# Window attention, block pipeline: the q and k matmuls of the convolution slots uncut

## The chip, the cores and the metric

The kernel runs on one core of a Trainium2 chip. A core has TensorE (PE, with its weight loads shown as PEld), VectorE (DVE), ScalarE (ACT), GpSimd (POOL) and SyncE (SP, which here only issues DMAs). The metric is the device time of one execution in microseconds.

## The reference

The input is an image of 511 x 511 tokens with 192 channels in bf16. A depthwise 3x3 convolution of it is added to it, the result is normalised over the channels, and windows of 7 x 7 tokens go through attention with 4 heads of 48 channels; the projected output is added to the image after the convolution.

```python
    for i in range(kk):
        for j in range(kk):
            pe = pe + xp[:, i:i + H, j:j + W, :] * dw_pe[i, j][None, None, None, :]
    x0 = x + pe
    h = _layernorm(x0, axis=-1)
    ...
    qkv = (hw @ w_qkv).reshape(-1, ws * ws, 3, nh, dh)
    ...
    attn = jnp.einsum('wnhd,wmhd->whnm', q, k) * scale
    attn = _softmax(attn, axis=-1)
    out = jnp.einsum('whnm,wmhd->wnhd', attn, v)
    out = out.reshape(-1, ws * ws, C) @ w_o
    ...
    return x0 + out
```

There are 73 x 73 windows.

## The kernel before

**Blocks and slots.** The windows are cut into 42 blocks of up to 128. A block is worked in slots of 8 windows (`CH = 8`, 49 tokens each, `TOK = 392`), 16 slots for a full block, 667 in all. While the slots of block b run their attention, the same slots also convolve block b+1, normalise and transpose it, and project block b-1 out. The order of all this is written out by hand in the loop at lines 561 to 665 of `fast`; no scheduler changes it, and each engine runs its instructions in that order, waiting on semaphores.

**One slot** has these stages on PE, in this order:

- A, q (line 378, `stage_A`): the transposed tokens `HO` of 8 windows are multiplied by the two halves of the head-padded `Wqk`, with 96 + 96 channels accumulated in two matmuls (`kt`). ACT copies the result to `q` (386).
- E (461, `stage_E`): the attention output of two slots earlier is transposed back; DVE copies it to `HO` (462).
- A, k: as for q, with ACT's copy to `k`.
- V (394, `stage_V`): eight matmuls of 192 columns, ACT copies to `v` (402).
- projections (473, `proj`) of block b-1, two or three in each of slots 2 to 6: eight matmuls of 192 columns each, a copy on ACT to `pO` (484), an addition to `X` on POOL (488).
- D (437, `stage_D`): attention weights times v of the previous slot; DVE normalises (446, 447).
- B (416, `stage_B`): the logits; ACT takes the exponential into `pt` (424).
- in later slots, transposes of the normalised rows of block b+1 (354), copied to `HO` by DVE or ACT (364).

All of A, E, V, D, B and the projections take their PSUM tile in turn from one rotation of three (`PS`), so a stage can start only when the copy out of the tile three uses back is done.

**The convolution** (`conv_mm`, 314 to 324) is one matmul per channel: the 81 values of a window's padded 9 x 9 patch for 128 windows are the stationary operand (`XP`, one channel out of 192, so its elements lie 192 apart), and 49 columns of a filter matrix `T` stream through. Every ten channels DVE adds the PSUM tile (one of two, `psc`) to `X` (324). These matmuls are not a stage of their own. They are placed between the matmuls of A and V by `fill(weight)` (597): each call adds a share of the slot's quota and issues as many convolution matmuls as the quota allows. A whole slot has weight 24: 8 for q, 8 for k, 8 for v. The quota of a block's 192 channels is spread over its first seven slots, 27 or 28 channels in each of the first six and 7 in the seventh. When the next block's convolution is finished and its loads are issued, the last slot convolves 20 channels of the block after that "ahead" (`ahead`, 590), placed by `fill` in the k and v stages.

**The cut.** In a slot with convolution left to do, and not in an "ahead" slot, `stage_A` issues each of its four products as two matmuls of 196 columns (`cuts = 2`, line 594), with `fill(1)` after each. In all others it issues one of 392 columns with `fill(2)` after it. The weights of a product are loaded again for the second half, since the two accumulation steps (`kt`) alternate.

**Loads and stores.** SP issues the patches `XP` of block b+2 once the convolution of block b+1 is done (there is one `XP`), then the tokens `X` of block b+2 (255) into the tile that block b-1 has left, and the stores of block b-1 (303) between them.

Of the kernel before, what the change touches and what calls it, by code (L numbers as in the profile page):

```python
# [32 lines left out]
WS, NH, C, DH, S = 7, 4, 192, 48, 49  # L33
BLK, CH, KP, KT = 128, 8, 81, 96
TOK = CH * S
# [27 lines left out]
class _Kernel:  # L63
# [194 lines left out]
    def fast(self, ctx):  # L258
# [4 lines left out]
        HO = [pool.tile([128, 2, BLK, 64], BF, name=f"HO{i}") for i in range(2)]  # L263
# [26 lines left out]
        mm = nc.tensor.matmul  # L290

        def two_bank(ps, ncol):
            return ps[:].rearrange("p (b n) -> p b n", b=2)[:, :, 0:ncol]
# [20 lines left out]
        def conv_mm(cv):  # L314
            c = cv.c
            if c % 10 == 0:
                cv.ps = PCB.next()
            mm(cv.ps[:, (c % 10) * S : (c % 10 + 1) * S], lhsT=XP[0:KP, :, c], rhs=T[0:KP, c, :], start=True, stop=True)  # L318
            cv.c += 1
            if cv.c % 10 == 0 or cv.c == C:  # L320
                c0 = c - c % 10
                n = cv.c - c0
                xv = self.X[cv.b % 3][:, :, c0 : c0 + n]
                nc.vector.tensor_tensor(out=xv, in0=cv.ps[:, 0 : n * S].rearrange("p (c s) -> p s c", s=S), in1=xv, op=ALU.add)  # L324
# [43 lines left out]

        def stage_A(b, ck, which, fill, cuts=1):
            dst = (q_, k_)[which]
            ps = PS.next()
            m = CH // cuts
            for ab in range(2):
                for i in range(cuts):
                    for kt in range(2):
                        mm(  # L378
                            ps[:, ab * 512 + i * m * S : ab * 512 + (i + 1) * m * S],
                            lhsT=self.Wqk[kt][0:KT, which * 2 + ab, :],  # L380
                            rhs=HO[b % 2][0:KT, kt, ck * CH + i * m : ck * CH + (i + 1) * m, 0:S],
                            start=(kt == 0),
                            stop=(kt == 1),
                        )
                        fill(2 / cuts)
            nc.scalar.copy(out=dst[:, :, 0:TOK], in_=two_bank(ps, TOK))  # L386

        def stage_V(b, ck, fill, eng, v_):
            ps = PS.next()
            for pi in range(4):  # L390
                w = ck * CH + 2 * pi
                col = (pi // 2) * 512 + (pi % 2) * C
                for kt in range(2):
                    mm(  # L394
                        ps[:, col : col + C],
                        lhsT=HO[b % 2][0:KT, kt, w : w + 2, :].rearrange("p w s -> p (w s)"),
                        rhs=self.Wv[kt][0:KT, :],
                        start=(kt == 0),
                        stop=(kt == 1),
                    )  # L400
                    fill(1)
            eng(  # L402
                out=v_[:].rearrange("p (b j) h e -> p b (j h) e", b=2)[:, :, :, 0:DH],
                in_=two_bank(ps, 2 * C).rearrange("p b (g d) -> p b g d", d=DH),
            )
# [142 lines left out]
        n = Next(0)  # L548
# [12 lines left out]
        for g in range(NG + LE + 1):  # L561
            b, ck = groups[g] if g < NG else (NB, g - NG)
# [5 lines left out]
            if ck == 0:  # L568
                n = nn if nn else Next(b + 1) if b + 1 < NB else None
# [9 lines left out]
            def part(lo, hi, total, at=None):  # L579
                return min(total, max(0, int(((f if at is None else at) - lo) / (hi - lo) * total + 0.5)))  # L580
# [7 lines left out]
            conv = n.conv if n else None  # L588
            conv_goal = base + part(0.0, 0.39 + d, C - base)
            ahead = n and conv.c == C and n.tr == WS and early and xpn == len(xp) and xln == len(xl)  # L590
            if ahead:
                conv, conv_goal = nn.conv, 10 * part(0.875, 1.0, 2)
            conv_start = conv.c if n else 0
            cuts = 2 if n and conv.c < conv_goal and not ahead else 1
            quota = [0.0]

            def fill(weight):
                quota[0] += (conv_goal - conv_start) * weight / (16 if ahead else 24)
                while n and quota[0] >= 0.999 and conv.c < conv_goal:
                    quota[0] -= 1.0  # L600
                    conv_mm(conv)
# [4 lines left out]
            def hook(share):  # L606

                nonlocal xpn, xln
                at = f0 + (f - f0) * share
                if n and n.conv.c == C:  # L610
                    n.stats(int(s_start + (s_goal - s_start) * share))
                while sq and sq[0][0] <= g + share:
                    _, bb, k = sq.pop(0)
                    store(bb, k)
                    stored[bb] = k + 1
                if n is None or n.conv.c == C:
                    goal = part(0.38 + d, 0.96 if many else 0.66 + 0.5 * d, len(xp), at)
                    while xpn < goal:
                        xp[xpn]()
                        xpn += 1  # L620
                    if b < 1 or stored.get(b - 1, 0) == len(CHUNKS):
                        goal = part(0.62 - 0.5 * d, 0.82, len(xl), at)
                        while xln < goal:
                            xl[xln]()
                            xln += 1

            if g < NG:
                stage_A(b, ck, 0, fill if not ahead else lambda w: None, cuts)
            if 0 <= g - LE < NG:
                stage_E(*groups[g - LE], nc.vector.tensor_copy)  # L630
            if g < NG:
                hook(0.3)
                stage_A(b, ck, 1, fill, cuts)
                hook(0.5)
                stage_V(b, ck, fill, nc.scalar.copy, vv[g % 2])
                while n and conv.c < conv_goal:
                    conv_mm(conv)
                hook(0.7)
# [275 lines left out]
```

## Time and profile before

| | |
|---|---|
| median of three runs | 3874.21 us (3873.48 to 3881.06) |
| the profiled execution | 3874.21 us, span 3872.5 us |
| mean granted TensorE clock | 0.938 |
| matmuls of 196 columns in A (line 378) | 4688 |
| matmuls of 392 columns in A (line 378) | 2992 |
| convolution matmuls (line 318) | 8064 |

One execution is profiled. Each instruction is shown with its engine, its line, and its tiles as written<-read. A matmul's length is modelled and includes its way through the array, so matmuls overlap in the listing; the distance between the starts of two tells how long the first one held the engine. A weight load may run beside the matmul before it. "Granted clock" is the share of TensorE's full speed that it was given. A wait is put down to the instruction that ended last before it. In an answer by intervals each line has the interval and its length, then busy time and number of instructions of PE, PEld, DVE, ACT and POOL, the granted clock, the busy share of the DMA engines and GB/s.

### The profile page before, as it was taken

To read this page: it belongs to the slowest core of one execution; us is meant where nothing else is said; L and a number is where in the kernel's file an instruction comes from. 1 tells how busy PE (TensorE), PEld (TensorE's weight loads), DVE (VectorE), ACT (ScalarE), POOL (GpSimd) and SP (SyncE) were. 2 spreads that over 40 slices of the span, in tenths; PEclk is the share of its full clock that TensorE was granted. 3 is DMA by queue.
4 is the path that set the end of the run, shared out by engine and by line. 5 is a ranking of instruction groups with operands and counts; after the bars stand their busy time and mean duration, and the time that the engine had idled before them with its cause. 6 is when DMAs were issued, how large, how long until landed. Compare 5 with 4: busy or idle time off the path is not lost.

```text
span 3872.5 us, 170289 instructions
## 1 busy us (share of the span) xinstructions
PE 3447.8 (89%) x77393; PEld 3052.7 (79%) x77393; DVE 2496.1 (64%) x4236; ACT 2790.3 (72%) x3512; POOL 2046.9 (53%) x1425
## 2 busy tenths in 40 slices
PE   4999999999999999999999999999999998888777
PEld 3888887888888888888888888888888887777665
DVE  6766666766666666667666666677666665555553
ACT  1777777877777777778777777778777776666665
POOL 4355565655555555555555555566555555455543
PEclk9989999999999999989899999999899988889988
DMA  5244344444333444444433344444433334444311
GB/s 136 69 101 100 97 113 103 111 104 109 98 94 94 106 104 111 105 102 117 103 94 94 94 103 104 109 116 111 107 98 94 94 94 94 93 94 93 62 34 43
DMA packets 529124, 377.40 MB, mean 97 GB/s; under 512 B 453595, under 2 KB 453787, under 8 KB 528393
## 3 DMA queue, kind: packets, MB, share of 16 engines
q1 hardware_dynamic: 521440, 363.75, 38.8%
q8 instruction: 607, 9.95, 1.1%
q10 hardware_dynamic: 6953, 2.69, 0.3%
q14 instruction: 124, 1.02, 0.1%
HBM read 265.31 MB, written 100.27 MB: 94 GB/s over the span
## 4 chain that ended last, share of the span: by engine, by line
PE 54%; DVE 16%; ACT 12%; DMA 6%; POOL 5%; issue 3%; SPq 3%; ACTq 0%; DVEq 0%; POOLq 0%
PE ps L378 20%; PE ps L394 9%; ACT pO L484 8%; PE psc L318 8%; PE ps L461 7%; DVE bnst L329 5%; PE ps L473 5%; DMA X<-in_x_dram 4%; DVE o L447 4%; POOL X L488 4%; DVE HO L364 3%; PE psc L354 3%; ACT v L402 2%; DVE HO L462 2%; PE ps L437 2%
## 5 line engine op out<-in xcount | busy, mean ns | idle before, releaser
L488 POOL TENSOR_TENSOR X<-X,pO 128x768 bf16<-128x768 bf16 (+1 forms) x539 | 830.0, 1561 | 1617.9 <-ACT pO L484 1604.0
L378 PE MATMUL ps<-HO,Wqk 96*128 96x196 bf16 (+1 forms) x7680 | 1400.5, 295 | 172.6 <-ACT pO L484 146.5
L318 PE MATMUL psc<-T,XP 81*128 81x49 bf16 x8064 | 1082.1, 210 | 104.6 <-DVE X L324 49.3
L318 PEld LDWEIGHTS <-XP 81*128 81x128 bf16 x8064 | 1045.1, 175 | 156.2 <-issue 143.5
L378 PEld LDWEIGHTS <-Wqk 96*128 96x128 bf16 x7680 | 781.6, 107 | 240.4 <-issue 117.7
L386 ACT CAST k<-ps 128x784 bf16<-128x784 f32 x667 | 542.2, 813 | 388.8 <-PE ps L378 330.8
L324 DVE TENSOR_TENSOR X<-psc,X 128x490 bf16<-128x490 f32 x840 | 534.3, 643 | 337.6 <-PE psc L318 234.1
L386 ACT CAST q<-ps 128x784 bf16<-128x784 f32 x667 | 542.3, 813 | 271.9 <-PE ps L378 236.9
L344 POOL TENSOR_TENSOR h<-X,rstd 128x1344 bf16<-128x1344 bf16 x287 | 697.8, 2431 | 22.5
L394 PE MATMUL ps<-Wv,HO 96*128 96x192 bf16 x5336 | 670.0, 251 | 26.4 <-ACT q L386 21.1
L447 DVE TENSOR_TENSOR o<-ps,rs 128x768 bf16<-128x768 f32 x667 | 638.7, 958 | 23.5
L394 PEld LDWEIGHTS <-HO 96*128 96x128 bf16 x5336 | 531.6, 106 | 128.6 <-issue 95.2
L402 ACT CAST v<-ps 128x768 bf16<-128x768 f32 x667 | 536.1, 804 | 114.2 <-PE ps L394 110.8
L424 ACT ACTIVATE pt<-ps 128x784 bf16<-128x784 f32 x667 | 550.4, 825 | 76.8 <-PE ps L416 57.8
L462 DVE COPY HO<-ps 96x784 bf16<-96x784 bf16 x667 | 380.9, 571 | 328.3 <-PE ps L461 326.3
L446 DVE RECIPROCAL rs<-ps 128x16 f32<-128x16 f32 x667 | 168.1, 252 | 632.7 <-PE ps L437 548.5
L329 DVE BATCH_NORM_STATS2 bnst<-X 128x6 f32<-128x384 bf16 x1050 | 533.7, 546 | 2.2 <-DVE X L324 0.5
L484 ACT CAST pO<-ps 128x768 bf16<-128x768 f32 x498 | 386.0, 798 | 130.8 <-POOL X L488 87.0
L461 PEld LDWEIGHTS <-o 128*96 128x96 bf16 x5336 | 395.2, 133 | 95.2 <-DVE o L447 57.8
L461 PE MATMUL ps<-ident,o 128*96 128x128 bf16 x5336 | 451.4, 232 | 18.3 <-DVE o L447 17.4
L339 POOL TENSOR_TENSOR rstd<-rstd,expo 128x7 f32<-128x7 f32 x294 | 439.6, 1495 | 24.5
L473 PE MATMUL ps<-Wo,HO 96*128 96x192 bf16 x4116 | 435.2, 260 | 1.3 <-DVE HO L462 0.7
(55 smaller groups left out, 2876.9 us busy)
## 6 DMA issues: line engine op xcount, KB each, us to landing
XP<-in_x_dram SPq DMA_DIRECT2D x644, 216.0 KB
X<-in_x_dram SPq DMA_DIRECT2D x574, 168.0 KB
out_dram<-X SPq DMA_DIRECT2D x246, 336.0 KB
XP<-in_x_dram SPq DMA_DIRECT2D x71, 212.6 KB
out_dram<-X SPq DMA_DIRECT2D x82, 168.0 KB
XP<-in_x_dram SPq DMA_DIRECT2D x12, 192.0 KB
X<-in_x_dram SPq DMA_DIRECT2D x9, 165.4 KB
XP<-in_x_dram SPq DMA_DIRECT2D x42, 30.4 KB
```

What stands on the lines that cost most here:

```text
L318: mm(cv.ps[:, (c % 10) * S : (c % 10 + 1) * S], lhsT=XP[0:KP, :, c], rhs=T[0:KP, c, :], start=True, stop=True)
L329: nc.vector.bn_stats(out=bnst[:, s : s + 2, :].rearrange("p a f -> p (a f)"), in_=self.X[b % 3][:, s : s + 2, :].rearrange("p s c -> p c s"),)
L344: eng.tensor_tensor(out=h[:, :, :], in0=self.X[b % 3][:, t, :], in1=rstd[:, t].unsqueeze(2).to_broadcast([128, WS, C]), op=ALU.mult)
L378: mm(ps[:, ab * 512 + i * m * S : ab * 512 + (i + 1) * m * S], lhsT=self.Wqk[kt][0:KT, which * 2 + ab, :], rhs=HO[b % 2][0:KT, kt, ck * CH ...
L386: nc.scalar.copy(out=dst[:, :, 0:TOK], in_=two_bank(ps, TOK))
L394: mm(ps[:, col : col + C], lhsT=HO[b % 2][0:KT, kt, w : w + 2, :].rearrange("p w s -> p (w s)"), rhs=self.Wv[kt][0:KT, :], start=(kt == 0) ...
L402: eng(out=v_[:].rearrange("p (b j) h e -> p b (j h) e", b=2)[:, :, :, 0:DH], in_=two_bank(ps, 2 * C).rearrange("p b (g d) -> p b g d", d=DH),)
L447: nc.vector.tensor_tensor(out=o_[:].rearrange("p b q (h d) -> p b (q h) d", d=DH), in0=ov[:, :, :, 0:DH], in1=r_[:].rearrange("p (b g) -> ...
L461: mm(ev, lhsT=o_[:, sl, Q, kt * KT : (kt + 1) * KT], rhs=ident[:], start=True, stop=True, is_transpose=True)
L473: mm(ps[:, col : col + C], lhsT=HO[b % 2][0:KT, kt, :, s0 + i], rhs=self.Wo[kt][0:KT, :], start=(kt == 0), stop=(kt == 1))
L484: nc.scalar.copy(out=o[:].rearrange("p (b s) c -> p b (s c)", b=2), in_=two_bank(ps, 2 * C))
L488: nc.gpsimd.tensor_tensor(out=xv, in0=xv, in1=o[:, 0:n, :], op=ALU.add)
```

## The change

The cut is taken out. `stage_A` loses its parameter `cuts` and always issues four matmuls of 392 columns, with `fill(2)` after each, in the slots with convolution too. `fill` and the quotas stay as they were, so the same convolution matmuls are issued in the same slot, in groups of two or three after each long matmul of q and k instead of one or two after each half. Stage V and everything else is as before.

```diff
-        def stage_A(b, ck, which, fill, cuts=1):
+        def stage_A(b, ck, which, fill):
             dst = (q_, k_)[which]
             ps = PS.next()
-            m = CH // cuts
             for ab in range(2):
-                for i in range(cuts):
-                    for kt in range(2):
-                        mm(
-                            ps[:, ab * 512 + i * m * S : ab * 512 + (i + 1) * m * S],
-                            lhsT=self.Wqk[kt][0:KT, which * 2 + ab, :],
-                            rhs=HO[b % 2][0:KT, kt, ck * CH + i * m : ck * CH + (i + 1) * m, 0:S],
-                            start=(kt == 0),
-                            stop=(kt == 1),
-                        )
-                        fill(2 / cuts)
+                for kt in range(2):
+                    mm(
+                        ps[:, ab * 512 : ab * 512 + TOK],
+                        lhsT=self.Wqk[kt][0:KT, which * 2 + ab, :],
+                        rhs=HO[b % 2][0:KT, kt, ck * CH : (ck + 1) * CH, 0:S],
+                        start=(kt == 0),
+                        stop=(kt == 1),
+                    )
+                    fill(2)
             nc.scalar.copy(out=dst[:, :, 0:TOK], in_=two_bank(ps, TOK))
...
-            cuts = 2 if n and conv.c < conv_goal and not ahead else 1
             quota = [0.0]
...
-                stage_A(b, ck, 0, fill if not ahead else lambda w: None, cuts)
+                stage_A(b, ck, 0, fill if not ahead else lambda w: None)
             if 0 <= g - LE < NG:
                 stage_E(*groups[g - LE], nc.vector.tensor_copy)
             if g < NG:
                 hook(0.3)
-                stage_A(b, ck, 1, fill, cuts)
+                stage_A(b, ck, 1, fill)
```

## The prediction

> **What bounds the kernel now.** I read first the page's busy shares and its chain, then the chain inside one slot that carries both convolution and projections, then the matmuls' starts there.
>
> ```profile
> span 3872.5 us, 170289 instructions
> ...
> PE 3447.8 (89%) x77393; PEld 3052.7 (79%) x77393; DVE 2496.1 (64%) x4236; ACT 2790.3 (72%) x3512; POOL 2046.9 (53%) x1425
> ...
> PE 54%; DVE 16%; ACT 12%; DMA 6%; POOL 5%; issue 3%; SPq 3%; ACTq 0%; DVEq 0%; POOLq 0%
> ```
>
> PE is the busiest engine and holds more than half of the chain that ended last. The slot from 1087.26 to 1093.65, in the chain of waits (start, length, what):
>
> ```profile
> 1087.26 0.25 PE ps L378
> ...
> 1088.48 0.47 PE ps L461 x8
> ...
> 1091.19 0.80 PE ps L473 x8
> ...
> 1092.06 0.70 ACT pO L484
> ...
> 1092.80 0.81 ACT pO L484
> ...
> 1093.65 0.25 PE ps L378
> ```
>
> From 1087.26 to 1091.19 everything in the chain is PE's q, transpose-back, k and v stages with the convolution between them. Then come one projection, two copies on ACT, and the next slot's q stage, which waits for the PSUM buffer that the second copy frees. PE idles 0.30 us there, but that idle time begins after the stages above, so it cannot hide anything that lengthens them. The same holds in a slot without projections: its next q stage waits for the copy of v, which follows the v stage.
>
> **The change, part by part.** The caption's other items (weights loaded ahead, rows normalised last) are the same in both files. Only the halving goes: in slots with convolution left to do, a q or k stage issued eight matmuls of 196 columns with about one convolution matmul after each; now it issues four of 392 with two or three after each. Total columns are equal. By the two programs' instruction orders, 4688 halves become 2344 wholes (293 slots x 8), so 2344 matmuls and 2344 weight loads go. DVE, ACT, POOL and SP have the same instructions, waits and order in both, so no DMA and no queue entry moves.
>
> The price stands in the trace of before twice: the cut form in the slot above, and the uncut form in a block's last slot, where 20 channels are convolved ahead without cutting. First the cut form, then the uncut one, then the uncut one at half clock (start, modelled length, work):
>
> ```profile
> 1087.74 0.25 PE L378 MATMUL ps<-HO,Wqk 96*128 96x196 bf16 x1
> ...
> 1087.87 0.25 PE L378 MATMUL ps<-HO,Wqk 96*128 96x196 bf16 x1
> 1087.95 0.29 PE L318 MATMUL psc<-T,XP 81*128 81x49 bf16 x2
> 1088.09 0.25 PE L378 MATMUL ps<-HO,Wqk 96*128 96x196 bf16 x1
> ...
> 967.14 0.33 PE L378 MATMUL ps<-HO,Wqk 96*128 96x392 bf16 x1
> 967.31 0.37 PE L318 MATMUL psc<-T,XP 81*128 81x49 bf16 x3
> 967.52 0.34 PE L378 MATMUL ps<-HO,Wqk 96*128 96x392 bf16 x1
> 967.70 0.28 PE L318 MATMUL psc<-T,XP 81*128 81x49 bf16 x2
> 967.82 0.34 PE L378 MATMUL ps<-HO,Wqk 96*128 96x392 bf16 x1
> ...
> 613.87 0.51 PE L378 MATMUL ps<-HO,Wqk 96*128 96x392 bf16 x1
> 614.17 0.29 PE L318 MATMUL psc<-T,XP 81*128 81x49 bf16 x2
> 614.29 0.50 PE L378 MATMUL ps<-HO,Wqk 96*128 96x392 bf16 x1
> ```
>
> Matmul lengths are modelled and overlap, so I use the distance from one start to the next. A half followed by one convolution matmul takes 0.13 us here (median 0.123), by two 0.22: the second adds 0.09, because its weight load has only a 49-column matmul to hide under, while the first one's hides under the 196 columns. A whole followed by two takes 0.30 and by three 0.38. So the same work, two halves with one each, takes 0.246, against 0.300 as a whole with two.
>
> Medians over all such rows at full clock: half with 0, 1, 2 behind it 86, 123, 215 ns; whole with 0, 2, 3: 170, 300, 384 ns. A whole with one has no row; I take 208 (170 plus the 37 that one adds to a half), between 190 (49 more columns at the whole's 0.43 ns each) and 262 (the 92 that a third adds); with 158 of them, the ends move the sum by 9 us at most.
> Halves: 498 x 86 + 3686 x 123 + 504 x 215 = 605 us.
> Wholes: 170 x 170 + 158 x 208 + 1512 x 300 + 504 x 384 = 709 us. Difference +104 us.
> At half clock, halves 162, 205, 257; wholes 327, about 375, 419, 512 (few rows). Same sum: 966 against 1006, +41 us. Of the halves with one behind them 17% ran at half clock (600 of 3450), so 0.83 x 104 + 0.17 x 41 = **+93 us of PE time**.
>
> What hides part of it: in a block's first slot the convolution stalls until X has landed and DVE is late with it; the transpose-back waits for DVE there ("0.26 <-DVE o L447" before 1061.68). The q stage's share there, about 0.2 us in 34 blocks, is covered: -6 us. In the other slots no such wait stands before it. The X landing itself does not absorb more: its chain of DMA issues starts when the convolution ends, and so moves with it. Direct part: **+87 us**.
>
> The 2344 weight loads removed are worth nothing by themselves: the 36 ns from a convolution matmul to the next half is already in the 123. [...]
>
> The second term is the clock. It drops to half for 3.41 us or a multiple after a stretch in which PE streamed little:
>
> ```profile
> 351.93:356.50 4.57, 4.43 (x124) 4.39 (x123) 3.61 (x7) 3.25 (x4) 0.00 (x0) 1.00 0.02 5
> 3476.45:3483.43 6.98, 6.98 (x122) 6.87 (x122) 3.70 (x7) 3.25 (x4) 0.00 (x0) 0.50 0.01 2
> 718.22:721.63 3.41, 2.05 (x80) 1.94 (x80) 1.21 (x2) 2.40 (x4) 2.56 (x2) 1.00 0.02 5
> 721.63:725.04 3.41, 3.41 (x34) 3.41 (x34) 1.25 (x2) 1.44 (x2) 2.27 (x2) 0.50 0.00 0
> ```
>
> The first two lines are a block's second slot at clock 1.00 and 0.50 (the clock stands after the five engines' busy times): 4.57 and 6.98 us. The other two show a drop after a stretch with PE busy 2.05 of 3.41. Counting columns, the clock came back after stretches that were almost filled at half rate, and stayed down where they were a few per cent emptier. At half clock two halves with one each carry 490 columns in 410 ns, the whole with two 490 in 419, with three 539 in 512 (before 462). Wholes thus leave the array emptier, and some stretches should last longer. Half clock falls in the first five slots of the blocks for 353 of 484 us, in 37 stretches. A unit of 3.41 us more costs about 1.04 us. For a slot of 27 channels, some 18.4 of them among the halves, grows by 0.41 us at full clock (13.6 x 123 + 2.4 x 215 against 5.6 x 300 + 2.4 x 384 ns) and by 0.17 at half: 4.98 and 7.15 us, and 3.41 x (1 - 4.98/7.15) is 1.04. Lower end: ten units fewer, because blocks of another length meet the 3.41 us steps elsewhere: -10 us. Upper end: two more units per stretch: 77 us. I take three quarters of a unit each, 29 us, since most returns to full clock here were narrow.
>
> Sum: 3872.5 span plus 1.7 around it is the profiled run's 3874.2, the same as the median of the three runs. 3874 + 87 + 29 = **3990 us**.
>
> **The rivals.**
> *Faster, because the long matmul hides all the loads behind it.* If the convolution loads ran ahead under 392 columns, a whole with two would take its streaming time, 490 x 0.434 = 213, with one 191, with three 234: 500 us instead of 605 at full clock, 87 less after the 0.83: 3787. It decides from the point where a whole with two takes under 246. Against it stand the 0.30 and 0.38 above.
> *Hidden.* If another engine set the slot's end, nothing would move: 3874. For it: PE waits 146.5 us in all for the projection copies. Against: those copies start behind the lengthened stages.
> *The clock stays down longer.* Two more units in each stretch, and six more drops of three units after slots with three projections: 77 + 19: 3874 + 87 + 96 = 4057. For it: at half clock the wholes with three fill only 539 of 614 possible columns. Against: the v stage and the projections still fill the array there.
> *The clock drops less*: 3874 + 87 - 10 = 3951.
>
> **How the numbers follow.** My forecast, 3960 to 4025, has 0.62; the longer half clock 0.2; the clock dropping less 0.1; hidden 0.04; faster 0.04. The range 3940 to 4065 takes in the forecast and both clock cases. A measurement tells about 0.2%, 8 us, from no change. Faster by more: 0.04; within: 0.03; slower: 0.93.
>
> **What would show it.** In the profile after: 5336 matmuls of one width in the q and k group, and 0.30 and 0.38 us between their starts in the slots that were cut; the second slot near 4.98 us at full clock, slots with two projections near 6.75 instead of 6.35; ACT's waits for the q and k matmuls up; the mean granted clock slightly under 0.938. Wrong would be: 0.25 us between those starts (the loads ran ahead), or the idle time before a q stage shrinking by what the stages grew.

## The result, and the profile after

The changed kernel takes 4102.05 us (median of four runs, 4090.62 to 4104.47), beside 3874.09 us before (four runs, 3873.48 to 3881.06): a ratio of 1.0578, 95% interval 1.0555 to 1.0601. It is slower, as forecast, but by 228 us where 116 were forecast, and 37 us above the upper end of the range.

The page of the kernel after: span and instructions, busy times of the engines, the granted clock in 40 slices, and the shares of the chain that ended last.

```profile
span 4102.8 us, 165601 instructions
...
PE 3704.7 (90%) x75049; PEld 3173.1 (77%) x75049; DVE 2501.9 (61%) x4236; ACT 2795.2 (68%) x3512; POOL 2045.3 (50%) x1425
...
PEclk9888988998978889998888988998899988988878
...
PE 58%; DVE 13%; ACT 10%; DMA 7%; POOL 4%; issue 3%; SPq 3%; ACTq 0%; DVEq 0%; POOLq 0%
```

DVE, ACT and POOL do the same work as before, to 6 us. PE has 2344 matmuls fewer and is busy 257 us longer, with its share of the chain up from 54% to 58%. The mean granted clock is 0.878 where it was 0.938: in 40 slices the row of the clock has more eights than it had before, where it read

```profile
PEclk9989999999999999989899999999899988889988
```

The matmuls of one slot at full clock, then of one at half clock (start, modelled length, work), in the kernel after:

```profile
1608.65 0.33 PE L376 MATMUL ps<-HO,Wqk 96*128 96x392 bf16 x1
1608.82 0.28 PE L318 MATMUL psc<-T,XP 81*128 81x49 bf16 x2
1608.94 0.33 PE L376 MATMUL ps<-HO,Wqk 96*128 96x392 bf16 x1
...
1609.53 0.33 PE L376 MATMUL ps<-HO,Wqk 96*128 96x392 bf16 x1
1609.70 0.37 PE L318 MATMUL psc<-T,XP 81*128 81x49 bf16 x3
1609.91 0.29 PE L459 MATMUL ps<-ident,o 128*96 128x128 bf16 x2
...
665.37 0.50 PE L376 MATMUL ps<-HO,Wqk 96*128 96x392 bf16 x1
665.67 0.39 PE L318 MATMUL psc<-T,XP 81*128 81x49 bf16 x3
665.88 0.43 PE L459 MATMUL ps<-ident,o 128*96 128x128 bf16 x2
```

By the distances between starts, a whole with two convolution matmuls holds the array for 0.29 us at full clock (1608.94 less 1608.65), with three for 0.38. At half clock the whole with three takes 0.51. These are the durations that the prediction read from the last slot of the blocks before.

Stretches of the kernel after: the interval and its length, busy time of PE, its weight loads, DVE, ACT and POOL, and the granted clock. The first two are a block's second slot at full and at half clock, the other two a stall and what came behind it.

```profile
1608.65:1613.61 4.96, 4.83 (x116) 4.76 (x116) 3.63 (x7) 3.25 (x4) 0.00 (x0) 1.00 0.02 3
664.11:671.33 7.22, 7.22 (x123) 6.05 (x116) 3.71 (x7) 3.25 (x4) 0.00 (x0) 0.50 0.01 2
1219.75:1223.16 3.41, 1.96 (x23) 1.84 (x22) 2.39 (x5) 1.15 (x2) 0.00 (x0) 1.00 0.00 0
1223.16:1260.71 37.55, 37.55 (x522) 32.06 (x521) 15.46 (x26) 17.15 (x22) 8.09 (x5) 0.50 0.08 20
```

The second slot takes 4.96 us at full clock, where it was 4.57. The last two lines are the main reading. PE was busy 1.96 of 3.41 us, and the clock fell to half. It then stayed there for 37.55 us, 11 steps of 3.41, although by the profile PE was busy in all of them. The step is read from the traces' records of the clock: 72 of this kernel's 73 stretches at half clock, and 67 of 68 before, last 3.413 us or a whole multiple of it; the one left over in each trace runs past the last instruction.

What stalled PE in the third stretch, from the timeline (in brackets the idle time before, and what ended it):

```profile
1220.00 1.24 DVE L324 TENSOR_TENSOR X<-psc,X 128x490 bf16<-128x490 f32 x2 [3.54 <-DMA X<-in_x_dram]
1220.72 0.28 PE L318 MATMUL psc<-T,XP 81*128 81x49 bf16 x2 [1.15 <-DVE X L324]
```

It is the block's first slot. The 20 channels convolved ahead fill both `psc` tiles. DVE can't add them to `X` before the tokens land, and PE waits for DVE. Before the change this stall was there too: DVE waited 74.5 us for the tokens in all, and 106.2 after it.

Where the time went, by a tally of the traces (us at half clock, by slot of the block, each number rounded by itself; one unit is 3.41 us):

| slots | before | after | change of the slots' time |
|---|---|---|---|
| 0 | 176 | 217 | |
| 1 | 72 | 172 | |
| 2 | 20 | 156 | |
| 3 | 68 | 214 | |
| 4 and 5 | 18 | 162 | |
| 0 to 5 together | 353 | 922 | +257 |
| 6 | | | +2 |
| 7 | 88 | 45 | -20 |
| 8 to 15 | | | -9 |
| all | 484 | 1004 | +230 |

In slots 0 to 5, 569 us more ran at half clock, 167 units. The longer groups cost some 90 us of the 257 there (the full-clock differences of the slots: 4.57 to 4.96 in slot 1, 8.20 to 8.58 in slot 2, and 6.31, 6.40, 6.32 to 6.67, 6.77, 6.67 in slots 3 to 5). The remaining 167 us over 167 units are 1.0 us each; PE's idle time in these slots is no part of it, it fell by 16 us. Stretches of half clock that begin in these slots rose from 37 to 56, and their mean length from 2.76 to 4.82 units; the longest has 14.

### The profile page after: what moved, and what is told of

It is laid out like the page before. It is cut to its first block, busy times and chain, and to the rows that moved or that the text cites. A ratio compares the mean times of both kernels' runs of the same rounds, so it can differ in the third digit from the quotient of the medians.

```text
span 4102.8 us, 165601 instructions
## 1 busy us (share of the span) xinstructions
PE 3704.7 (90%) x75049; PEld 3173.1 (77%) x75049; DVE 2501.9 (61%) x4236; ACT 2795.2 (68%) x3512; POOL 2045.3 (50%) x1425
## 4 chain that ended last, share of the span: by engine, by line
PE 58%; DVE 13%; ACT 10%; DMA 7%; POOL 4%; issue 3%; SPq 3%; ACTq 0%; DVEq 0%; POOLq 0%
PE ps L376 20%; PE psc L318 9%; PE ps L392 9%; PE ps L459 7%; ACT pO L482 6%; PE ps L471 6%; DMA X<-in_x_dram 6%; DVE bnst L329 5%; DVE o L445 4%; POOL X L486 3%; PE ps L435 3%; PE psc L354 2%; PE ps L414 2%; SPq L239 2%; DVE HO L364 2%
## 5 line engine op out<-in xcount | busy, mean ns | idle before, releaser
L376 PE MATMUL ps<-HO,Wqk 96*128 96x392 bf16 x5336 | 1493.9, 366 | 147.8 <-ACT pO L482 126.7
L318 PEld LDWEIGHTS <-XP 81*128 81x128 bf16 x8064 | 1127.0, 176 | 299.4 <-issue 182.4
L318 PE MATMUL psc<-T,XP 81*128 81x49 bf16 x8064 | 1113.2, 226 | 108.4 <-DVE X L324 59.9
L392 PE MATMUL ps<-Wv,HO 96*128 96x192 bf16 x5336 | 706.1, 259 | 22.3 <-ACT q L384 20.4
L376 PEld LDWEIGHTS <-Wqk 96*128 96x128 bf16 x5336 | 564.5, 112 | 207.7 <-issue 81.4
L392 PEld LDWEIGHTS <-HO 96*128 96x128 bf16 x5336 | 549.5, 110 | 122.2 <-issue 84.1
L459 PEld LDWEIGHTS <-o 128*96 128x96 bf16 x5336 | 418.9, 139 | 96.3 <-DVE o L445 56.2
L459 PE MATMUL ps<-ident,o 128*96 128x128 bf16 x5336 | 473.6, 239 | 21.1 <-DVE o L445 20.1
L471 PE MATMUL ps<-Wo,HO 96*128 96x192 bf16 x4116 | 476.8, 276 | 1.3 <-DVE HO L460 0.7
```

The source lines that it names most:

```text
L376: mm(ps[:, ab * 512 : ab * 512 + TOK], lhsT=self.Wqk[kt][0:KT, which * 2 + ab, :], rhs=HO[b % 2][0:KT, kt, ck * CH : (ck + 1) * CH, 0:S], ...
L392: mm(ps[:, col : col + C], lhsT=HO[b % 2][0:KT, kt, w : w + 2, :].rearrange("p w s -> p (w s)"), rhs=self.Wv[kt][0:KT, :], start=(kt == 0) ...
L459: mm(ev, lhsT=o_[:, sl, Q, kt * KT : (kt + 1) * KT], rhs=ident[:], start=True, stop=True, is_transpose=True)
L471: mm(ps[:, col : col + C], lhsT=HO[b % 2][0:KT, kt, :, s0 + i], rhs=self.Wo[kt][0:KT, :], start=(kt == 0), stop=(kt == 1))
```

## The experiments

The theory after the result: the groups of two and three cost some 90 us directly, and the rest comes from half clock, whose stretches last longer where the array is less filled. Rivals: the width of the long matmuls or the fewer weight loads do it; any lengthening of the slots moves the blocks against the 3.41 us steps and does it; the longer groups cost more than their full-clock rows show.

### Groups without wholes

The halves stay, but the convolution matmuls are placed after every second one, in groups of two and three.

```diff
-                        fill(2 / cuts)
+                        if cuts == 1 or kt == 1:
+                            fill(2)
```

> The kernel before with its halves of 196 columns and all its weight loads, but the convolution matmuls come only after every second half, two or three at a time as in the changed kernel. Theory (the time comes from weight loads that have only a 49-column matmul to hide under, and from a half clock that lasts longer because such slots fill the array less): 4060 to 4130 us, half clock about 1000 us as in the changed kernel. Rival (the width of the matmuls or the number of weight loads does it): 3870 to 3900 us, half clock near 484 us.

Measured: 4078.21 us, 1.0524 of before (1.0463 to 1.0584). Half clock rises from 484 to 784 us, less than the 1000 expected. The windows of a second slot at full clock and one at half clock:

```profile
2349.82:2354.83 5.01, 4.88 (x123) 4.83 (x123) 3.63 (x7) 3.25 (x4) 0.00 (x0) 1.00 0.01 3
754.84:762.08 7.24, 7.24 (x130) 7.00 (x124) 3.71 (x7) 3.25 (x4) 0.00 (x0) 0.50 0.01 2
```

The slot takes 5.01 and 7.24 us, as with the wholes (4.96 and 7.22), though its matmuls and loads are as many as before and 196 columns wide. So the grouping carries 204 of the 228 us with the width and the number of weight loads as they were; neither of these is needed for the loss. The matmuls show how:

```profile
2349.82 0.33 PE L378 MATMUL ps<-HO,Wqk 96*128 96x196 bf16 x2
2349.99 0.28 PE L318 MATMUL psc<-T,XP 81*128 81x49 bf16 x2
2350.12 0.33 PE L378 MATMUL ps<-HO,Wqk 96*128 96x196 bf16 x2
```

Two halves and two convolution matmuls in this order take 0.30 us, as a whole with two does; in the order half, one, half, one they took 0.246.

### As long at full clock, but with a filled array

To the halved kernel, two matmuls of 99 columns are added behind each of the two outputs (`ab`) of q and of k in the slots with many channels, into unused PSUM columns. The second slot becomes nearly as long as in the kernel after, with work that fills the array.

```diff
+                if cuts == 2 and many_conv[0]:
+                    for kt in range(2):
+                        mm(
+                            ps[:, ab * 512 + TOK : ab * 512 + TOK + 99],
+                            lhsT=self.Wqk[kt][0:KT, which * 2 + ab, :],
+                            rhs=HO[b % 2][0:KT, kt, ck * CH : ck * CH + 3, 0:33],
+                            start=True,
+                            stop=True,
+                        )
...
+            many_conv[0] = conv_goal - conv_start > 15
...
```

> The kernel before plus eight more matmuls of 99 columns in each slot with more than 15 convolution matmuls (2016 in 252 slots, written to spare PSUM columns that nobody reads): about the same PE time added per slot as the change adds, 0.36 us, but with the array full. Theory (the second part of the loss is a half clock that lasts because the array is emptier): 252 x 0.36 = 91 us more at most 110, 3960 to 3985 us, half clock not above 500 us. Rival (any lengthening of these slots draws the clock down): 4080 to 4130 us, half clock near 1000 us.

Measured: 3959.18 us, 1.0213 (1.0176 to 1.0251), with 483 us at half clock against 484. A second slot at full clock and one at half:

```profile
1813.03:1817.94 4.91, 4.78 (x132) 4.73 (x131) 3.60 (x7) 3.25 (x4) 0.00 (x0) 1.00 0.02 3
3565.62:3573.23 7.61, 7.61 (x130) 7.50 (x130) 3.69 (x7) 3.25 (x4) 0.00 (x0) 0.50 0.01 2
```

The slot is 0.34 us longer than before at full clock. In the 252 slots with the addition that makes 86 us, and the kernel lost 85. So the slots may grow without more half clock in all, which is against the rival that any lengthening does it. In one respect the rival holds: in slots 0 to 5 this kernel has 50 stretches where the kernel before has 37 (426 us against 353), and slot 7 has 14 us where it had 88. Longer slots alone move the drops about; but with the array filled the stretches are short (2.42 units), and the sum stays. Beside the grouped halves (5.01 us, 4078) this slot is only 0.10 us shorter, some 25 us in 252 slots, and the kernel 119 faster; its half clock is 301 us less, 88 units, and at 1.0 us each, an estimate, that is most of the difference. In a slot that does fall to half clock the addition is dear, 7.61 us against 7.24: what it buys is shorter stretches, 2.42 units on the mean against 4.18 there.

### As long, but emptier

One matmul of 49 columns with strided weights from `T` is added behind each of these outputs instead.

```diff
+                if cuts == 2 and many_conv[0]:
+                    mm(
+                        ps[:, ab * 512 + TOK : ab * 512 + TOK + S],
+                        lhsT=T[0:KP, 0:128, 0],
+                        rhs=T[0:KP, 0, :],
+                        start=True,
+                        stop=True,
+                    )
```

> The kernel before plus four more matmuls of 49 columns with a strided weight load in each such slot (1008 in all, to spare PSUM columns that nobody reads), each behind a convolution matmul, so that its load is exposed: about 0.37 us per slot with an almost empty array. Theory: 93 us directly plus a longer half clock, 4020 to 4110 us, half clock 750 to 1000 us. Rival (the clock did not follow from the array's filling): 3960 to 3985 us, half clock near 484 us.

Measured: 3947.76 us, 1.0175 (1.0114 to 1.0236), far under what was expected. The dose had been misjudged twice. The q stage grew by 0.13 us (1.08 to 1.21), so the slot by 0.26 and not 0.37, and the added 49 columns fill the array themselves (the stages reach 0.973 in the table below, where the kernel after has 0.933). Half clock rose to 616 us all the same, by 132 us or 39 units, where the denser and longer addition raised it by none. The direction speaks for the theory; the size is no test of it.

### What ends a stretch at half clock

From the rows at half clock I worked out how full the q and k stages of the convolution slots were: their columns over 1.2 per ns (392 columns in 327 ns, a bare whole at half clock) times the stages' length (medians, slots 1 to 5). Beside it stands the mean length of the stretches that begin in slots 0 to 5; the kernels with an even spread, with convolution behind projections, without loads of `X` and with nothing ahead are described below.

| kernel | filled | stretches | mean units | half clock in slots 0 to 5, us |
|---|---|---|---|---|
| dense addition | 1.00 | 50 | 2.42 | 426 |
| halves, even spread | 0.992 | 38 | 2.42 | 323 |
| before | 0.986 | 37 | 2.76 | 353 |
| halves, some behind projections | 0.985 | 23 | 2.87 | 225 |
| sparse addition | 0.973 | 50 | 3.22 | 550 |
| wholes, even spread | 0.960 | 28 | 4.29 | 410 |
| grouped halves | 0.936 | 51 | 4.18 | 723 |
| after | 0.933 | 56 | 4.82 | 922 |
| halves, no loads of X | 0.973 | 31 | 1.35 | 143 |
| wholes, no loads of X | 0.943 | 23 | 4.00 | 297 |
| halves, nothing ahead | 0.985 | 12 | 3.33 | 137 |
| wholes, nothing ahead | 0.940 | 13 | 3.85 | 171 |

In the upper eight kernels, which all have the stall on `X`, the length rises as the array empties: 2.4 to 2.9 units above 0.98, 4.2 to 4.8 under 0.965. From the kernel before to the kernel after the filling falls by 0.053, and the mean stretch grows from 2.76 to 4.82 units. In the lower four, which have fewer stretches, halves and wholes differ in the same direction, but halves alone do not fall in order (1.35 at 0.973, where 8 of the 13 rows are of the emptier k stage; 3.33 at 0.985 with 12 stretches).

Read unit by unit, the traces show behind which units the clock came back. For each 3.41 us I added up the columns that streamed, each matmul weighted by the rows of its weights as the traces show them, as a share of 128: 96 for q, k, v and projections, 81 for the convolution, 128 for transposes; the small products of D and B, with weights of 49 x 64 and 48 x 64, count a quarter. 4096 columns of 128 rows, which are 3.413 us at half clock's measured 1.2 per ns, count as 1. Over the twelve traces, without the unit that ends each program:

| state | weighted sum of the unit | units | followed by the other clock |
|---|---|---|---|
| half | under 0.72 | 780 | 0 |
| half | 0.72 to 0.77 | 508 | 259 |
| half | over 0.77 | 358 | 356 |
| full | under 0.72 | 564 | 564 |
| full | 0.72 to 0.76 | 121 | 49 |
| full | over 0.76 | 10416 | 2 |

The value that divides these units best is near 0.745 in both states. The weights were chosen after the event because they divide the units well: at half clock the sum puts 94% of them right, columns without the weighting by rows 83%. The stretch of eleven units shown above began behind a unit of 0.62, ran through units of 0.66 to 0.75, and ended after one of 0.755. This is why a small lack decides here: by this count, at 1.2 columns per ns, a stage of q, k, v or the projection reaches 96/128 = 0.75 at half clock and no more, the convolution 81/128 = 0.63, and only the transposes (128 columns in 107 ns) lie above. The median unit at half clock in slots 1 to 5 has 0.755 before, 0.730 after, 0.730 with grouped halves and 0.769 with the dense addition.

### Moving convolution behind the projections

Before, 8 or 16 channels of a slot with projections are moved singly behind matmuls of its second and third projection, so that q, k and v carry fewer.

```diff
+            late = min(8 * max(0, len(pj) - 1), conv_goal - conv_start) if n and not ahead and conv_goal < C else 0
+            conv_goal -= late
...
+            for i, s0 in enumerate(pj):
+                proj(b - 1, s0, b == NB and s0 % 8 == 0, one if i else lambda: None)
...
```

Here `one` issues one convolution matmul after each of the projection's.

> The kernel before, cut, but in the slots with projections 8 or 16 of the convolution matmuls stand one by one behind the matmuls of the second and third projection instead of among the halves and V. Theory (a convolution matmul behind a long matmul costs 37 to 40 ns, behind another one 92, and PE idles 0.3 to 1.8 us after the projections): 40 a block leave the path of the q, k and v stages, 40 x 40 blocks x 0.046 = 74 us less, 3770 to 3810 us, half clock in the fourth slot lower. Rival (projections are on the path themselves, ACT sets the slot's end): 3860 to 3890 us.

Measured: 3845.53 us, 0.9939 (0.9903 to 0.9976); a gain, but 35 us short of the expected range. Half clock fell to 339 us, in slot 3 from 68 to 6, so that part went as meant. The price of the new place was wrong:

```profile
1065.14 0.30 PE L473 MATMUL ps<-Wo,HO 96*128 96x192 bf16 x1
1065.28 0.20 PE L318 MATMUL psc<-T,XP 81*128 81x49 bf16 x1
1065.32 0.31 PE L473 MATMUL ps<-Wo,HO 96*128 96x192 bf16 x1
```

A projection matmul with one convolution matmul takes 0.18 us; the bare one takes 0.092. The pair adds 0.09 and not the 0.037 of a half. Here the short distance is the one behind the convolution (0.04) and the long one that behind the projection (0.14): the projection's matmul streams 192 columns, and its weights are themselves strided (in the trace of before its loads take 179 ns in the median and the convolution's 173, where those of q and k take 100 and those of v 98). The pair's 0.18 is twice the 0.09 of a load with only a 49-column matmul to hide under, and the projection's strided load has just that; the reading fits, no run tests it by itself. So slots 3 to 5 grew to 6.47, 6.63 and 6.46 us (6.31, 6.40, 6.32), and only slot 2 gained, from 8.20 to 7.78.

### An even spread, with halves and with wholes

The channels of a block are spread so that the slots with few projections carry 24, and slot 2 gets 40 of which 16 go behind its projections, where they cover PE's gap at the end of that slot (1.4 us before, median; the 1.8 of the expectation is too long). The same edit was made to the kernel before and to the kernel after; in the latter each whole then has exactly two convolution matmuls behind it.

```diff
+            even = n and base == 20 and not ahead and plain(b + 1)
+            if even:
+                conv_goal = base + (24, 48, 88, 112, 136, 160, 172)[min(ck, 6)]
+            late = 16 if even and len(pj) == 3 and ck == 2 else 0
...
```

> The kernel before, cut, with the convolution of the next block spread so that in nearly every full block each half and each matmul of V has one convolution matmul behind it and no two (24 in a slot), 16 more of the third slot behind its second and third projection, where PE waited 1.8 us, and 12 in the seventh. Theory: 3.6 convolution matmuls at 92 ns leave each of five slots, and the third slot's idle time is filled: about 1.9 us a block, 68 us, plus some 25 us because the clock no longer drops before the fourth slot: 3770 to 3810 us, half clock 300 to 400 us. Rival (the doubled ones were hidden): 3860 to 3875 us.

> The changed kernel, uncut, with the same even spread: each whole matmul has exactly two convolution matmuls behind it, hardly ever three. At half clock such a group fills the array for 490 of 503 possible columns (0.419 us), one with three for 539 of 614 (0.512 us). Theory (emptiness at half clock keeps it there, and the threes are the emptiest): the direct cost against the cut even kernel stays, 6 slots x 8 x 54 ns = 2.6 us a block, 93 us, but the clock adds less than 40 us: 3860 to 3920 us, half clock 350 to 550 us. Rival (uncut slots draw the clock down whatever the groups are): 3960 to 4040 us, half clock 800 us or more.

Measured: 3834.30 us with halves (0.990, 0.987 to 0.993) and 3913.83 with wholes (1.0089, 1.0057 to 1.0122). The uncut form loses 80 us here instead of 228: without the threes, and with the gap covered, its half clock is 485 us instead of 1004. That is as expected. The halves missed their range. Their slots 3 to 5 went down to 6.03 to 6.06 us, but slot 0 took 34 us more in all, because the stall on `X` grew, from 74.5 us before to 120.3 (DVE's wait for the tokens; us in total, times, longest us):

```profile
DVE X L324 <- DMA X<-in_x_dram: 120.3, 30, 7.1
```

The chain of DMA issues that brings the tokens takes some 41 us from the end of a block's convolution, in this kernel as in the others that load `X` (to the last issue 41.0 us in the median, in the trace of before and in that of after). It does not get faster when the block does.

### The stall itself: no loads of X

From the third block on `X` is not loaded, so nothing waits for it. Again once with halves, once with wholes.

```diff
-                xl, xln = (list(load_x(b + 2)), 0) if b + 2 < NB else ([], 0)
+                xl, xln = [], 0
```

> The kernel before without the loads of the tokens X from the third block on (the convolution is added to what the tile holds, so those blocks are computed from other data): no wait for X at the start of a block. Theory (half-clock stretches of the first slot begin because PE waits there for X): the first slots lose their stall and most of their half clock, 3740 to 3800 us, half clock 200 to 300 us. Rival (they begin for another reason): 3800 to 3840 us, half clock above 400 us.

> The changed kernel, uncut, with the same loads left out. Theory (the change costs 91 us directly, and the rest because stretches that begin at a stall last longer): with one of the two kinds of stall gone, the loss against the cut kernel without these loads is 130 to 170 us instead of 228: 3880 to 3960 us, half clock 350 to 550 us. Rival (the clock falls in uncut slots by themselves): the loss stays near 228 us, 3970 us or more, half clock 700 us or more.

Measured: 3736.67 us with halves (0.9633, 0.9581 to 0.9685), just under the expected range, and 3815.58 with wholes (0.982, 0.9754 to 0.9886). The stall and its clock cost the halved kernel 137 us. The loss by the change falls from 228 to 79 us, under the 130 to 170 expected, and half clock is 350 us with wholes (1004 with the stall) although the array is filled to 0.943 only. So in these runs a filling of 0.94 did its harm where something started a stretch, and half clock of the size of the kernel after came only with both. Of the smallness of the 79, part may be chance: in the two profiled executions slots 0 to 5 differ by 133 us (1610 and 1743), and slot 7, with 22 drops against 2, gave 37 back. The edit also takes the loads' traffic away; the next pair does not.

### Nothing ahead

`early` off: no channels are convolved ahead, so both `psc` tiles are free when a block begins and the first addition to `X` comes later. The 192 channels are spread as above, with 28 or 26 in a slot, 40 in slot 2.

```diff
-                early = nn and plain(b + 2)
+                early = None
...
+            even = n and b and plain(b + 1)
+            if even:
+                conv_goal = base + (28, 56, 96, 122, 148, 174, 192)[min(ck, 6)]
+            late = 16 if even and len(pj) == 3 and ck == 2 else 0
...
```

> The cut even kernel without the 20 channels convolved ahead in a block's last slot: those 20 go to the block's own first seven slots (28, 28, 40, 26, 26, 26, 18 channels), so X is needed only when the first ten channels of the next block's first slot are done. Theory (the first slot's stall on X costs itself and the half clock behind it): most of the stall goes, A to E in the first slot 1.2 to 2 us instead of about 3.4 on the mean, half clock 200 to 300 us, 14 more doubled channels a block at 55 ns cost 28 us, 3740 to 3800 us. Rival (DVE waits for X as long as before and holds the transpose-back): 3830 to 3870 us.

> The cut kernel without the channels ahead, made uncut and nothing else: the change of this study, made where PE hardly stalls at the start of a block. Theory (the change costs 2.2 to 2.6 us a block directly, and the clock only what its stretches leave to lengthen): 90 to 105 us more than the cut one, plus at most 30 for the clock, 3820 to 3865 us, half clock 250 to 350 us. Rival (an uncut slot draws the clock down by itself): 3930 us or more, half clock 500 us or more.

Measured: with halves 3731.41 us, 0.9626 (0.9588 to 0.9664), 143 us faster than the kernel before and faster than the expected range; with wholes 3810.26, 0.9812 (0.9767 to 0.9858). DVE's wait for the tokens with halves, then with wholes:

```profile
DVE X L324 <- DMA X<-in_x_dram: 16.5, 6, 6.0
```

```profile
DVE X L324 <- DMA X<-in_x_dram: 12.4, 6, 4.0
```

The wait falls from 120.3 us (halves, even spread) to 16.5. Half clock is 241 us with halves and 227 with wholes, and no longer differs. The spread also covers PE's gap here, in both. What is left of the change is its direct cost: 79 us in the medians, 69 in the spans of the two profiled executions. The second slots of both at full clock:

```profile
1608.65:1613.32 4.67, 4.55 (x125) 4.51 (x124) 3.60 (x7) 3.25 (x4) 0.00 (x0) 1.00 0.01 4
```

```profile
1542.23:1547.30 5.07, 4.93 (x116) 4.88 (x116) 3.62 (x7) 3.25 (x4) 0.00 (x0) 1.00 0.01 3
```

The slot is 0.40 us longer uncut, as it was with the stall (4.57 to 4.96). The page of the faster kernel shows where its gain over the kernel before comes from:

```profile
span 3731.3 us, 170289 instructions
...
PE 3363.8 (90%) x77393; PEld 2962.1 (79%) x77393; DVE 2496.5 (67%) x4236; ACT 2794.7 (75%) x3512; POOL 2050.7 (55%) x1425
...
PEclk9999999999999999999999999999999998988888
```

PE has as many matmuls as before and is busy 84 us less; 243 us less at half clock, 71 units, account for most of that at 1.0 us each. The rest of the gain is PE's idle time, 57 us less: some 37 of it before slot 3, where the spread covers the gap, and 24 in slot 0, with the stall.

## Why the prediction was right in direction and too small

**The direct part held.** It was given as 87 us, from 0.246 against 0.30 us a pair and 0.38 with three. The rows after show 0.29 to 0.30 and 0.38, the second slot 4.96 where 4.98 was given, and slots with two projections 6.67 to 6.77 for "near 6.75". By the slots it is some 90 us; without the stall, the whole loss was 79 in the medians. That the long matmul might hide all loads behind it, or that another engine set the end, fell with these rows. The grouped halves, 0.30 us where the same work one by one took 0.246, agree with the mechanism named, that the second and third convolution load in a row has only 49 columns to hide under. The trace of before shows the order: in the group of three at 967.14 the convolution loads take 0.17 to 0.21 us, and each begins within 0.03 us of the start of the matmul ahead of it, the first beside the whole, the second and third beside a convolution matmul.

**The price of a unit held.** 1.04 us was given. The remainder of the tally gives 1.0, and the second slot's rows after give 3.41 x (1 - 4.96/7.22) = 1.07.

**The step that failed is the number of units.** "I take three quarters of a unit each" on 37 stretches gave 28 units and 29 us; 167 units came, some 167 us. The upper case, two units more in each stretch and six more drops of three units, 92 units, was still short. The mean stretch grew by 2.06 units, and on the old 37 that is 76: the upper case's size, not the chosen one's. The other 92 are 19 more stretches of 4.82. That the change would leave the number of stretches nearly as it was had been taken for granted; only its lower end reckoned with blocks that meet the 3.41 us steps elsewhere, and there as a gain.

**Why the stretches grew by more than taken.** The rival "the clock stays down longer" had the right mechanism, and was set against the remark that "the v stage and the projections still fill the array there". The tally says otherwise. Slots 2 to 5, with their v stages and projections, went from 106 to 532 us at half clock. By the weighted sum these matmuls take 96 of the 128 rows and reach 0.75 at most, hardly above the dividing 0.745, so they have nothing over with which to make up for emptier q and k stages. That the wholes with three fill only 539 of 614 possible columns was in the working already and should have decided: a slot that repeats a few times in a row gives every 3.41 us step the same small lack. In the experiments a filling of 0.933 against 0.986 went with 4.82 units against 2.76, and the dense addition, as filled as can be, brought the half clock back to what it was before.

**Why there were more of them.** Starts in slot 0 rose from 22 to 33, in slot 3 from 13 to 21. Most of this needs no emptier array: the dense addition, with slots nearly as long and filled, has 28 and 19, and 50 stretches of the 56. For slot 0 the traces show one cause. Slot 7 fell to half clock 20 times before, 6 times after and 4 times with the dense addition, because the blocks met the steps differently; without such a drop the later slots of the block are done sooner, and the tokens, whose last load is issued some 41 us behind the convolution's end, come later for PE. In the trace of before, the time up to the transpose-back of the next slot 0 is 2.25 us on the mean behind a slow slot 7, and a stretch begins there in 5 of 23 blocks; otherwise it is 3.83 us, and in 9 of 10. DVE's wait for the tokens, before and after (us in total, times, longest us):

```profile
DVE X L324 <- DMA X<-in_x_dram: 74.5, 22, 5.6
```

```profile
DVE X L324 <- DMA X<-in_x_dram: 106.2, 29, 6.2
```

So the prediction's remark that the landing of `X` "does not absorb more" was right, but the stall itself was not fixed: time won in a block's second half is given back there, with a drop of the clock behind it. For slot 3 the start lies behind PE's gap of 1.4 us at the end of slot 2; why more of its drops came there is not shown. Even spread and covered gap together brought the half clock of the wholes down to 485 us, and the two were not tried apart.

**What decided the size**, then, is what starts the stretches and the grouping together: 228 us with both as they were, 79 with the grouping but without the stall, 80 with the stall but in groups of two and with the gap covered. The halved kernel gains 137 us when the loads that cause the stall are gone.

## What to carry to other kernels

In this kernel short matmuls with strided weights stood best singly behind long ones whose weights are contiguous; a second one in a row cost 0.092 us where the first cost 0.037, and splitting a long matmul to make room paid for its additional loads (0.246 us against 0.30). Where a profile shows the clock at half behind a stall, price the stall with what follows it: look whether the work behind it is filled enough to end the stretch, counting rows of the weights as well as columns (that put 94% of the units at half clock right here, columns alone 83%), and take away the stall first. A change that empties the array by a few per cent (0.986 to 0.933 here, where 37 stretches of 2.76 units became 56 of 4.82) should be forecast with both the length and the number of half-clock stretches open, above all where every slot is alike.

## What the runs showed of the hardware beyond that

- A PE that the profile shows busy without a break did not by that bring the clock back. In the stretch above it was busy 37.55 of 37.55 us, eleven steps of 3.41, at 0.50. What divides the units of the twelve traces is the weighted sum of columns, near 0.745 of 4096, in both directions.
- A projection matmul of 192 columns with strided weights takes 0.092 us bare and 0.18 with one convolution matmul behind it. A half of 196 columns takes 0.086 and 0.123. The place behind a long matmul was not worth the same in both.
- In the dense addition useless columns cost only their own time (85 us for 2016 matmuls), with 483 us at half clock in all against 484. Taking 2344 loads and matmuls away, and grouping the convolution with it, cost 228.
